# Four blocks of group 0's first layer by seven products instead of eight, in a kernel whose five queues are written out by hand, and a new order for all of it

## The chip, the cores and the metric

The kernel runs on one core of one Trainium2 chip. The metric is the time of one execution in microseconds, as the device reports it; the time before is the median of three runs. One more execution was recorded by the hardware profiler: all the single durations in this document come from it.

The core has a matrix engine (PE, with its weight loads shown apart as PEld), a vector engine (DVE), a scalar or activation engine (ACT), a general engine (POOL, which also issues some transfers) and a queue engine that only issues transfers here (SP). Each engine runs its own instructions in the order in which they are written; engines wait for each other by semaphores only.

## The reference, cut to what matters

```python
scores = scale * np.matmul(q, k.transpose(0, 1, 3, 2))      # 8 x 12 heads, 448 x 448, head width 64
attn = np.maximum(scores, 0.0) ** 2 / S                     # no softmax: relu, then square
x = attn @ v, heads joined                                  # 3584 tokens x 768
h = x @ w_in                                                # 768 x 2048
g = h * (1.0 / (1.0 + np.exp(-1.702 * h)))
out = g @ w_out                                             # 2048 x 768, float32
```

Two parts follow each other: an attention whose weights are squared relus, and two dense layers with a gate between them. All matrix products run in 16 bits.

## The kernel before

The 96 heads are cut into 24 **units** of four heads (three units make the 448 tokens of one **group**, that is, one element of the batch; there are eight groups, 0 to 7). The second layer works on **pairs** of 128-token tiles, 14 pairs in all.

The function writes helpers and then one long list of short words (lines 431 to 600). Every word issues the instructions of one helper, and since the schedule is manual, the order of the words is the order in every engine's queue. A word is a name, its arguments, after `@` the PSUM banks (P0 to P7) that it takes, and after `:` the engine (`a` ACT, `d` DVE, `p` POOL) where that is not the usual one. The words that matter:

- `Lq u`, `Lk u`: SP loads a unit's q or k in 32 bits into the only buffer of its kind; `Q u`, `K u` cast it to 16 bits (usual engine: Q on POOL, K on ACT; DVE and the others where the word says so). `jq`, `jk`, `V`, `jwa`, `jwb`, `jo` are loads issued by POOL that cast on their way (q, k of units 1 to 5, all v, the weights).
- `tq u`, `tk u`: 7 or 14 transposes on PE (lines 117, 122); `eq`, `ek` bring the result from PSUM to SBUF.
- `s u.j`: four narrow score products, 64 x 64 weights each (line 141); `r u.j.a`: relu of one 128 x 448 half (line 152 on DVE, 154 on ACT); `x u.j`: the square of both halves (line 85 on DVE, 160 on ACT); `a u`: 28 narrow products with v (line 172), which need all seven squares of the unit; `e u.s`: the result to SBUF as the token-side operand `xb` of the first layer.
- `f g.f.r`: the plain way through the first layer, used for group 0 alone. One of 16 feature blocks of 128 is 6 products of 448 columns (line 208; r = 0, 1, 2 is the unit that gives the operand). `g g.f` is the gate from PSUM (ACT), `v g.f` widens the result into `ring`, the 16-bit input of the second layer (POOL or DVE).
- `u g.i.n`: the other way, used for groups 1 to 7. Four feature blocks (i = 0 to 3) are taken together as a 2 x 2 matrix of blocks and formed by **seven products** n = 0 to 6 instead of eight (Winograd's form of Strassen's method). Each n is 6 products of 224 columns (line 188, tile `hx`). They need sums of weight blocks (`S i.n`, DVE, once for all groups) and sums of token blocks (`T g.n`, DVE, four per group, two of them in place of their operand), and between the products partial results are saved and added: `t g.i.n` copies one PSUM bank (n = 0, 2, 4; ACT or DVE) and `b g.i.n` adds a second bank to such a copy (n = 1, 3, 6; DVE). Two banks are filled in two chains: u0, t0, u2, t2, u4, t4, u5, and u1, b1, u3, b3, u6, b6. b3 needs the copy t4, b6 the copy t2. Four gates `g g.i.n` and four widenings `v g.i.n` follow.
- `A m.n`, `p m.n`, `h m.n`, `l m.n`, `o m`: the second layer of a pair, also by seven products (8 of 384 columns each, line 188, tile `ox`), with four sums on DVE, copies `h` and last steps `l` into the output tile (lines 78, 82, 357), and the store on SP. `W c.n` are its weight sums on DVE, in four parts.

So a unit's work comes in on ACT and DVE (14 relus, 7 squares), and PE mixes four kinds of work: attention of later units, first layer and second layer of earlier groups. `m1` (line 202), `unit_product` (line 246), `t_sum` (line 236) and `from_bank` (line 352, whose engine is always DVE where a half is added to the output tile) are the helpers behind the words that the prediction counts.

Of the kernel before, what the change touches and what calls it, by code (L numbers as in the profile page):

```python
# [15 lines left out]
def kernel(  # L16
# [370 lines left out]
    with tc.manual_schedule():  # L387
# [34 lines left out]
        def zeros(e, p, n):  # L422
# [8 lines left out]
            "Lq0 Lk0 z9@0 jq1 jk1 I V0 V1 z1 Q0:d z1 z1 z1 z1 z1 z1 tq0@1 K0:d eq0:a tk0@2 ek0 "  # L431
            "tq1@3 jk2 eq1 s0.1@4.5 jq2 s0.4@6.7 s0.5@0.1 r0.1.1 r0.1.0:d s0.0@2.3 jq3 r0.5.1 "
            "r0.5.0:d s0.6@5.4 r0.0.0 r0.0.1:d r0.6.0 s0.2@1.0 x0.5 r0.2.0 s0.3@2.3 tk1@5 r0.2.1 "
            "x0.1 r0.4.0 ek1 jk3 r0.3.0 x0.2 r0.6.1 s1.6@1.0 jwb0 s1.3@6.5 r0.3.1:d r1.6.0 jwa0 "
            "r1.6.1 x0.6 s1.2@2.4 s1.0@3.1 r1.3.0 x0.3 r1.2.0 s1.5@0.6 x0.0 r0.4.1 r1.5.0:d r1.2.1 "
            "s1.1@2.7 r1.0.1 r1.0.0:d tk2@0 r1.1.0 x0.4 s1.4@4.1 r1.3.1 tq2@3 ek2 r1.1.1 a0@2.5 jq4 "
            "eq2 x1.3:a x1.2 jk4 r1.5.1 r1.4.0:d tq3@0 e0.0:a V2 x1.0 s2.3@7.3 e0.1:a tk3@6 jwb2 "
            "eq3 r2.3.1 s2.2@4.2 r1.4.1 ek3 s2.1@5.0 jwa2 r2.3.0 x1.1 s3.3@3.1 r2.1.1 jwa1 s2.4@6.7 "
            "x1.6 r2.2.0 jwb1 x1.4 r3.3.1 x1.5 a1@0.4 r2.1.0 jk5 r2.4.1 r3.3.0:d r2.2.1 jq5 "
            "s2.0@1.5 r2.4.0:d s3.2@7.3 e1.1:a f0.1.0@2 V3 e1.0 r2.0.0 s2.5@6.4 r2.0.1 r3.2.1:d "  # L440
            "jwb3 s3.4@0.1 r3.2.0 f0.1.1 r2.5.1:d r2.5.0 f0.0.0@5 jwa3 x2.2 f0.0.1 r3.4.0 V4 x2.0 "
            "s2.6@3.7 r3.4.1 s3.0@4.6 r2.6.0 x2.1 tk4@0 V5 r3.0.1 f0.2.0@1 r3.0.0:d r2.6.1 jo0.0 "
# [12 lines left out]
            "x5.3 V6 f0.12.0@1 r5.6.1 K6:d f0.14.0@5 v0.4 r5.2.1 f0.12.1 r5.6.0:d Lk7 x5.0:a "
            "u1.1.0@3 x5.1 u1.0.0@2 r5.2.0 x5.6 r5.4.0 f0.13.0@0 x5.5 u1.2.0@7 e4.1:a S3.1 x5.2:a "
            "f0.12.2 x5.4 f0.14.1 g0.12 a5@4.6 S3.3 Q6:d S1.2 Lq8 tq6@1 e5.0:a v0.12:d f0.13.1 T1.1 "
            "e5.1:a f0.14.2 t1.1.0:d tk6@4 g0.14 T1.2 f0.13.2 S0.3 u1.0.1@6 g0.13 S3.2 p0.0@5 "
            "t1.0.0 v0.13 eq6:a b1.0.1 v0.14 S1.4 u1.0.2 ek6:a S3.4 u1.1.1@0 g1.0.1 T1.3 u1.3.0@1 "
            "t1.0.2 b1.1.1 v1.0.1 u1.1.2 S1.3 g1.1.1 u1.0.4 W0.1 t1.1.2 u1.0.3 W2.1 t1.0.4 u1.1.4 "  # L460
            "K7 b1.0.3 u1.1.3 W1.1 g1.0.3 Lk8 f0.9.0@4 T1.4 t1.1.4 u1.0.6 v1.0.3 Q8:a b1.1.3 f0.9.1 "
            "v1.1.1 f0.9.2 b1.0.6 Lq7 u1.1.6 W3.1 g0.9 u1.3.1@6 g1.1.3 b1.1.6 v0.9 t1.2.0 u1.1.5 "
            "v1.1.3:d t1.3.0 A0.1@0 u1.2.1@4 g1.0.6 W2.3 u1.2.2 g1.1.6 v1.0.6 b1.2.1 tk7@0 t1.2.2 "
            "u1.0.5 b1.3.1 v1.1.6 W1.3 u1.3.2 g1.3.1 W0.3 g1.2.1 u1.2.4 v1.3.1 W3.2 t1.3.2 u1.3.3 "
            "t1.2.4 u1.2.3 A0.2@1 ek7:a u1.2.5 W3.3 g1.0.5 b1.2.3 u1.3.4 K8 v1.0.5 h0.0:d tq8@0 "
            "W2.2 u1.2.6 g1.2.5 Lk9 W1.2 eq8:a p0.1@2 v1.2.5 b1.2.6 W0.2 t1.3.4 v1.2.1 W2.4 "
            "s6.0@7.0 p0.2 r6.0.0 Q7 l0.1 g1.1.5 b1.3.3 r6.0.1 V8 s6.4@4.7 Lq9 W0.4 h0.2 s6.2@3.0 "
            "p0.3 A0.3 r6.2.0 r6.4.1 W3.4 r6.2.1 W1.4 r6.4.0 s6.5@3.7 v1.1.5:d tq7@0 r6.5.0 A0.4 "
            "p0.4 r6.5.1 eq7 x6.2:a x6.5 s6.6@4.3 x6.0 h0.4 s6.3@7.0 Q9 r6.6.1 u1.3.5 r6.3.1:d "
            "r6.3.0 tk8@3 l0.3 g1.3.5 p0.5 K9:p Lq10 r6.6.0:d x6.4:a ek8 v1.3.5 Lk11 x6.3:a "  # L470
            "s7.4@0.7 l0.5 s6.1@1.4 u1.3.6 r7.4.0 r6.1.1:d o1 r7.4.1 x6.6 s7.0@3.5 s7.1@0.4 r6.1.0 "
            "p0.6 b1.3.6 r7.0.1 x6.1 r7.1.0 r7.0.0 x7.4 s7.3@7.1 r7.1.1 s7.2@6.5 l0.6 a6@0.3 r7.2.0 "
            "x7.1 o0 r7.3.0 A2.1@0 r7.2.1 s7.6@4.2 x7.0 r7.3.1 s8.4@6.7 V10 tq9@5 r7.6.0 r7.6.1:d "
            "tk9@1 Q10 e6.1:a r8.4.0:d p2.0@4 eq9:a ek9 K11:p r8.4.1:d x7.2:a s8.2@2.3 x7.6 "
            "s7.5@6.5 Lk10 p2.1@1 r7.5.1 r7.5.0:d Lq11 e6.0:a x7.3 x7.5:a r8.2.0:d s8.1@7.5 a7@6.0 "
            "r8.2.1:d r8.1.1 r8.1.0 A2.2@1 h2.0 x8.1 s8.6@2.3 s8.3@5.7 e7.0:a p2.2 r8.3.0:d e7.1:a "
            "K10:p r8.6.0 r8.6.1:d r8.3.1 l2.1 V13 s9.0@6.5 Lk12 x8.6:a s8.0@0.2 x8.3 s8.5@3.7 p2.3 "
            "r8.0.0:d r8.0.1 r9.0.1 x8.2 r8.5.1 x8.0 tk11@0 r8.5.0 u2.1.0@2 x8.4 ek11:a x8.5 a8@5.7 "
# [152 lines left out]
```

## Time and profile before

| | us |
|---|---|
| median of 3 runs | 375.39 |
| lowest, highest | 374.13, 375.76 |
| the profiled execution, its own time | 374.8 |
| its span (first to last instruction) | 373.0 |
| PE busy | 365.6 (98%) |
| DVE busy | 321.5 (86%) |
| ACT busy | 297.3 (80%) |
| POOL busy | 114.3 (31%) |
| granted PE clock | 0.998 of full speed |

The profiled execution is 0.6 us below the median of the runs and inside their spread. Its span leaves 1.8 us of its own time outside. A matmul's row is its whole passage, and the next one enters before it has left; the price of a matmul in a row of many is therefore read from start to start, not from its duration. The same holds for DVE and ACT, whose instructions overlap by about 0.1 us.

### The profile page before, as it was taken

The page shows a single profiled execution, that of the slowest core. Times are in us where ns is not written, and L with a number is a line of the kernel's source. Part 1 is how long each engine was busy: PE and PEld are TensorE (multiplying, and loading weights), DVE is VectorE, ACT ScalarE, POOL GpSimd, SP SyncE. Part 2 cuts the span into 40 slices and gives each one's busy share as a digit, 9 for nine tenths or more (in the row PEclk, how much of TensorE's full clock was granted, in tenths as well). Part 3 has the DMA queues.
Part 4 walks back from the last instruction along what each step waited for, and adds up shares of the span by engine and source line. Part 5 has one row for each costly group of instructions (what it writes and reads, how often), then busy time and mean ns, then how long its engine had stood idle before and what let it go on. Part 6 is the DMA issues. An engine that isn't in the chain of part 4 may idle for free.

```text
span 373.0 us, 9514 instructions
## 1 busy us (share of the span) xinstructions
PE 365.6 (98%) x3830; PEld 252.9 (68%) x3830; DVE 321.5 (86%) x602; ACT 297.3 (80%) x568; POOL 114.3 (31%) x164
## 2 busy tenths in 40 slices
PE   8899999999999999999999999999999999999995
PEld 4444568855589555886568965599568855788663
DVE  3999999999999998898899699978998889767762
ACT  3999989999988999789978997899994897636310
POOL 6464523452334424231341322335400410012000
PEclk9999999999999999999999999999999999999999
DMA  9999999357673437360572524620520301110344
GB/s 195 171 188 206 238 232 232 135 138 203 166 196 99 120 62 209 112 160 2 134 199 34 177 28 114 183 37 2 95 43 2 86 2 41 45 44 16 71 99 114
DMA packets 31981, 43.16 MB, mean 116 GB/s; under 512 B 2368, under 2 KB 28608, under 8 KB 31936
## 3 DMA queue, kind: packets, MB, share of 16 engines
q1 hardware_dynamic: 14928, 28.06, 25.7%
q0 software_dynamic: 16608, 14.09, 25.2%
q8 instruction: 30, 0.49, 0.5%
q10 hardware_dynamic: 400, 0.39, 0.4%
q14 instruction: 15, 0.12, 0.1%
HBM read 45.61 MB, written 11.01 MB: 152 GB/s over the span
## 4 chain that ended last, share of the span: by engine, by line
PE 95%; DVE 3%; ACT 1%; issue 0%
PE ox L188 35%; PE hx L188 30%; PE sc L141 10%; PE av L172 8%; PE ht L208 5%; PE tr L117 4%; PE zp L426 1%; DVE at L85 1%; DVE at L152 1%; PE tr L122 1%; ACT at L154 1%; DVE kT L80 0%; DVE qT L80 0%; DVE osb L357 0%; DVE wT L417 0%
## 5 line engine op out<-in xcount | busy, mean ns | idle before, releaser
L154 ACT ACTIVATE at<-sc 128x448 f16<-128x448 f32 x229 | 112.2, 567 | 10.6 <-PE sc L141 9.9
L198 POOL TENSOR_SCALAR ring<-gf 128x448 f16<-128x448 f32 x87 | 53.7, 617 | 151.0 <-ACT gf L195 144.0
L188 PE MATMUL ox<-wout,ring 128*128 128x384 f16 x448 | 80.3, 326 | 0.0
L188 PEld LDWEIGHTS <-ring 128*128 128x128 f16 x568 | 53.0, 98 | 37.5 <-issue 7.6
L152 DVE TENSOR_SCALAR at<-sc 128x448 f16<-128x448 f32 x107 | 63.9, 617 | 5.8 <-PE sc L141 5.6
L85 DVE TENSOR_TENSOR at<-at 128x896 f16<-128x896 f16 x107 | 65.5, 636 | 1.7 <-ACT at L154 1.6
L188 PEld LDWEIGHTS <-win 128*128 128x128 f16 x672 | 63.8, 98 | 4.4 <-issue 2.1
L85 DVE TENSOR_TENSOR gf<-hx,gf 128x448 f32<-128x448 f32 x84 | 50.8, 620 | 9.9 <-PE hx L188 5.2
L160 ACT ACTIVATE at<-at 128x896 f16<-128x896 f16 x61 | 57.7, 960 | 0.5
L188 PE MATMUL hx<-xb,win 128*128 128x224 f16 x504 | 57.0, 259 | 0.0
L195 ACT ACTIVATE gf<-gf 128x448 f32<-128x448 f32 x84 | 47.2, 578 | 11.5 <-DVE gf L85 11.3
L141 PE MATMUL sc<-qT,kT 64*64 64x448 f16 x672 | 50.2, 359 | 1.6 <-DVE kT L80 1.1
L188 PEld LDWEIGHTS <-winS 128*128 128x128 f16 x504 | 48.0, 98 | 3.1 <-issue 1.3
L76 ACT ACTIVATE gf<-hx 128x448 f32<-128x448 f32 x60 | 31.8, 541 | 13.4 <-PE hx L188 11.4
L188 PE MATMUL ox<-wT,asum 128*128 128x384 f16 x224 | 40.6, 327 | 0.0
L188 PE MATMUL hx<-T,winS 128*128 128x224 f16 x336 | 39.7, 259 | 0.0
L172 PE MATMUL av<-at,v 64*64 64x448 f16 x672 | 36.2, 350 | 0.1
L141 PEld LDWEIGHTS <-kT 64*64 64x64 f16 x672 | 17.1, 105 | 23.9 <-issue 17.3
L188 PEld LDWEIGHTS <-asum 128*128 128x128 f16 x224 | 20.8, 98 | 16.6 <-issue 3.4
L357 DVE SCALAR_TENSOR_TENSOR osb<-ox,osb 128x384 f32<-128x384 f32 (+1 forms) x44 | 23.8, 541 | 5.9 <-PE ox L188 5.7
L78 ACT ACTIVATE osb<-ox 128x384 f32<-128x384 f32 x26 | 13.1, 503 | 19.6 <-PE ox L188 16.8
L172 PEld LDWEIGHTS <-v 64*64 64x64 f16 x672 | 20.4, 107 | 11.6 <-issue 1.5
(61 smaller groups left out, 426.0 us busy)
## 6 DMA issues: line engine op xcount, KB each, us to landing
out_dram<-osb SPq DMA_DIRECT2D x52, 192.0 KB, 3.0
qst<-in_q_dram SPq DMA_DIRECT2D x19, 448.0 KB, 4.5
kst<-in_k_dram SPq DMA_DIRECT2D x19, 448.0 KB, 4.2
v<-in_v_dram POOLq DMA_DIRECT2D x24, 224.0 KB, 5.0
win<-in_moe_w_in_dram POOLq DMA_DIRECT2D x8, 384.0 KB, 9.7
wout<-in_moe_w_out_dram POOLq DMA_DIRECT2D x4, 768.0 KB, 20.6
q<-in_q_dram POOLq DMA_DIRECT2D x5, 224.0 KB, 5.9
k<-in_k_dram POOLq DMA_DIRECT2D x5, 224.0 KB, 5.4
```

The costliest lines, as they stand in the source:

```text
L76: nc.scalar.activation(out=o, in_=i, func=AF.Copy)
L85: eng[e].tensor_tensor(out=o, in0=x, in1=y, op=op)
L141: nc.tensor.matmul(out=sc[a][c, 0:S], lhsT=st["kT"][r, j, c], rhs=st["qT"][r, :, c], start=True, stop=True)
L152: nc.vector.tensor_scalar(out=o, in0=i, scalar1=0.0, scalar2=None, op0=ALU.max)
L154: nc.scalar.activation(out=o, in_=i, func=AF.Relu)
L160: nc.scalar.activation(out=at, in_=at, func=AF.Square)
L172: nc.tensor.matmul(out=av[s][64 * a:64 * a + 64, 0:S], lhsT=v16[r, a, 64 * j:64 * j + 64], rhs=at[r, a, :], start=(j == 0), stop=(j == J - 1))
L188: nc.tensor.matmul(out=o, lhsT=lhs(i), rhs=rhs(i), start=start and i == 0, stop=i == n - 1, skip_group_check=True)
L195: nc.scalar.activation(out=o, in_=i, func=AF.Gelu_apprx_sigmoid, scale=1.0 / SC)
L198: eng[e].tensor_scalar(out=o, in0=i, scalar1=SC, scalar2=1.0, op0=ALU.mult, op1=ALU.mult)
L208: nc.tensor.matmul(out=hp[g, f][:, 0:S], lhsT=w[:, i, fo:fo + 128], rhs=xts[g][:, i, :], start=i == 0, stop=i == NK - 1)
L357: nc.vector.scalar_tensor_tensor(out=o, in0=x, scalar=1.0 / SC, in1=o, op0=ALU.mult, op1=ALU.add)
```

## The change

Feature blocks 12 to 15 of group 0 (the fourth set of four, i = 3) are no longer formed by the plain way, but by the seven products that the other groups use. Feature blocks 0 to 11 of group 0 stay as they are. For this the list gains `u0.3.0` to `u0.3.6` with their copies, adds, gates and widenings, and the four token sums `T0.1` to `T0.4`, which group 0 did not need before. The helpers are unchanged.

All other words are the same in kind but come in a new order, with other banks, and some work has another engine: over the whole program relus go 229 to 225 on ACT and 107 to 111 on DVE, copies `t` 60 to 57 on ACT and 24 to 30 on DVE, copies `h` 26 to 29 on ACT and 17 to 14 on DVE, widenings 41 to 35 on DVE and 87 to 93 on POOL, casts of k 4 to 6 on ACT and 13 to 11 on POOL, casts of q 4 to 3 on DVE and 12 to 13 on POOL, one `eq` from ACT to DVE.

The core of the diff (the places of group 0's fourth set):

```diff
-            "S2.3 g0.7 f0.15.0@2 f0.15.1 v0.6:d r5.1.1 v0.7 S0.4 f0.15.2 r5.1.0 s5.3@0.1 g0.11 "
...
-            "x5.3 V6 f0.12.0@1 r5.6.1 K6:d f0.14.0@5 v0.4 r5.2.1 f0.12.1 r5.6.0:d Lk7 x5.0:a "
-            "u1.1.0@3 x5.1 u1.0.0@2 r5.2.0 x5.6 r5.4.0 f0.13.0@0 x5.5 u1.2.0@7 e4.1:a S3.1 x5.2:a "
-            "f0.12.2 x5.4 f0.14.1 g0.12 a5@4.6 S3.3 Q6:d S1.2 Lq8 tq6@1 e5.0:a v0.12:d f0.13.1 T1.1 "
-            "e5.1:a f0.14.2 t1.1.0:d tk6@4 g0.14 T1.2 f0.13.2 S0.3 u1.0.1@6 g0.13 S3.2 p0.0@5 "
...
+            "u0.3.0@7 r5.2.0 u1.0.0@0 S0.3 g0.5 v0.5:d r5.3.1 x5.3 x5.1 r5.2.1 x5.6 u1.1.0@1 x5.2:a "
+            "Q6:a t1.0.0:d S1.4 u1.2.0@4 T1.1 K6:p tk6@2 a5@5.3 S1.3 e4.1:a e5.0:a e5.1:a u0.3.1@6 "
+            "T1.2 tq6@5 eq6:a T1.3 u1.0.1@3 S3.1 t0.3.0:d b1.0.1 b0.3.1 t1.1.0 v0.2 u1.0.2 t1.0.2 "
+            "ek6:a p0.0@5 u1.1.2 S3.3 S3.2 h0.0 u1.1.1@2 g1.0.1 Lk7 t1.1.2 V8 v1.0.1:d S3.4 u1.0.4 "
+            "g0.3.1 v0.3.1 t1.0.4 u1.0.3 b1.1.1 g1.1.1 u1.1.4 u1.1.3 b1.0.3 t1.1.4 g1.0.3 v1.1.1 "
+            "W2.1 u1.0.6 Lq8 Q8 b1.1.3 K7 g1.1.3 b1.0.6 v1.0.3 t1.2.0 T1.4 u1.1.6 b1.1.6 W3.1 "
...
+            "u1.3.3 W0.3 Lk8 g1.2.1 t1.2.4 W3.2 u1.2.3 u1.3.2 v1.2.1 g1.3.1 T0.1 T0.2 V7 t1.3.2 "
+            "b1.2.3 W2.2 u0.3.3 T0.3 u0.3.2 v1.3.1 t0.3.2 u1.2.6 u0.3.4 K8 b1.2.6 t0.3.4 W1.2 W0.2 "
+            "tk7@0 b0.3.3 W2.3 ek7:a g0.3.3 u1.3.4 Lq7 W2.4 u0.3.6 Q7:a b0.3.6 g0.3.6 v0.3.3 tq8@0 "
+            "u1.1.5 eq8 t1.3.4 v0.3.6:d u1.2.5 g1.2.5 s6.0@6.0 r6.0.1 v1.2.5 b1.3.3 r6.0.0:d u1.3.5 "
+            "T0.4 W3.4 tq7@4 g1.1.5 v1.1.5:d W1.4 s6.2@0.6 Lq9 r6.2.1 W1.3 u0.3.5 r6.2.0 Lk9 g0.3.5 "
+            "s6.5@1.6 r6.5.1 r6.5.0 u1.3.6 s6.4@0.7 v0.3.5:d r6.4.1 p0.1@6 s6.3@1.7 g1.3.5 x6.5:a "
+            "eq7 v1.3.5 Q9 s6.6@2.4 A0.1@0 A0.2@1 p0.2 x6.2:a K9 h0.2 r6.4.0:d r6.6.1 l0.1 r6.3.0:d "
```

## The prediction

> **What bounds the kernel now.** I read the page first: its busy shares and the chain of work that ended last.
>
> ```profile
> PE 365.6 (98%) x3830; PEld 252.9 (68%) x3830; DVE 321.5 (86%) x602; ACT 297.3 (80%) x568; POOL 114.3 (31%) x164
> ...
> PE 95%; DVE 3%; ACT 1%; issue 0%
> ```
>
> The chain names PE, but rows of a matmul overlap, so 98% does not say that PE was never held up. For that I read the timeline of PE, in which runs of equal matmuls are one line (start, length, count at the end), and took every price from start to start.
>
> ```profile
> 27.36 1.49 PE L172 MATMUL av<-at,v 64*64 64x448 f16 x28
> ...
> 31.67 0.76 PE L141 MATMUL sc<-qT,kT 64*64 64x448 f16 x12
> 32.36 2.44 PE L208 MATMUL ht<-xb,win 128*128 128x448 f16 x12
> 34.74 0.76 PE L141 MATMUL sc<-qT,kT 64*64 64x448 f16 x12
> ...
> 98.26 1.55 PE L172 MATMUL av<-at,v 64*64 64x448 f16 x28
> ...
> 332.99 1.46 PE L188 MATMUL ox<-wout,ring 128*128 128x384 f16 x8
> 334.29 0.74 PE L188 MATMUL hx<-xb,win 128*128 128x224 f16 x6
> 334.87 0.74 PE L188 MATMUL hx<-T,win 128*128 128x224 f16 x6
> ...
> 366.89 1.48 PE L188 MATMUL ox<-wT,ring 128*128 128x192 f16 x16
> ```
>
> Eight second-layer products take 1.30 us (332.99 to 334.29), six first-layer products of the seven-product form 0.575. Twelve plain first-layer products take 2.38 (32.36 to 34.74) and twelve score products 0.69. Comparing runs of 4, 8 and 12, a score word of four costs 0.188 and a plain product 0.19, and each passage between narrow (64 x 64) and full matmuls adds about 0.11, so one visit to the narrow ones costs 0.22. With 28 products of an attention at 1.32, seven transposes at 0.39 (the early, narrow 14 at 0.51) and the 16 products on zeros at the start 5.3, the sum over the program is: zeros 5.3, transposes 38 x 0.39 + 10 x 0.51 = 19.9, scores 168 x 0.188 = 31.6, attention 24 x 1.316 = 31.6, plain first layer 96 x 0.19 = 18.2, seven-product first layer 196 x 0.575 = 112.7, second layer 97 x 1.30 + 2 x 0.70 = 127.5, and 66 visits x 0.22 = 14.5: 361.3 us. PE runs from 1.12 to 368.37, 367.25 us, so 5.9 us are lost. The attention of unit 2 (the line at 27.36) stands 21.3 us into that sum, but starts 26.2 us after PE did: 4.9 of the 5.9 us are lost there, and only 1.0 in the 341 us behind it. So PE is the bound without gaps from 27 us on. Who holds it in the head is DVE, and I read DVE's timeline and two stretches (columns: length, then busy us of PE, PEld, DVE, ACT, POOL, clock, DMA).
>
> ```profile
> 26.70 2.22 DVE L85 TENSOR_TENSOR at<-at 128x896 f16<-128x896 f16 x4
> 28.84 0.62 DVE L80 COPY kT<-tr 128x896 f16<-128x896 f16 x1
> ...
> 46.86 0.39 DVE L198 TENSOR_SCALAR ring<-gf 128x448 f16<-128x448 f32 x1 [0.59 <-ACT gf L195]
> ...
> 96.97 2.22 DVE L85 TENSOR_TENSOR at<-at 128x896 f16<-128x896 f16 x4
> 99.11 0.68 DVE L85 TENSOR_TENSOR ring<-ring 128x1024 f16<-128x1024 f16 x1
> ```
>
> ```profile
> 28.84:99.11 70.27, 70.26 (x767) 45.13 (x764) 67.90 (x131) 67.01 (x132) 28.25 (x37) 1.00 0.92 194
> 99.11:140.00 40.89, 40.89 (x453) 29.24 (x446) 39.17 (x74) 35.75 (x69) 16.40 (x23) 1.00 0.49 124
> ```
>
> The last square of unit 2 ends at 28.84 and that of unit 8 at 99.11. Unit 8's attention starts at 98.26 and needs its squares one by one, 0.19 us apart, so the squares come in the nick of time. In these 70.27 us DVE is idle for 2.37 us, mostly short waits for ACT as at 46.86, and ACT for 3.26. PE is the bound, with DVE 3% and ACT 5% behind it. The change lands in this stretch.
>
> **The change part by part.** *Products.* Out: 4 blocks x 6 plain products x 0.19 = 4.56 us. In: 7 x 0.575 = 4.02. PE: -0.54.
>
> *Order on PE.* Counting in the two lists of words how often a score or attention word follows a full matmul gives 66 visits before and 69 after: +3 x 0.22 = +0.66. PE's own sum ends at +0.12; 30 visits instead of 26 lie before unit 8's attention, so its place moves by 4 x 0.22 - 0.54 = +0.34, and behind it PE has 0.22 less. The Trainium skill speaks against the change here: its page "TensorEngine Tiling (Array Packing)", section Tiling Modes, says that changing the tiling mode drains the engine. It gives no price; with free passages the forecast below would be 0.7 us lower.
>
> *Work on DVE and ACT between the two attentions.* Up to unit 2's attention the counts on DVE and on ACT are equal word for word in kind, so the head is taken as unchanged; the pieces only change places, which I bound by 0.5 us either way (DVE is never idle for over 0.1 us between 7.2 and 28.8). Up to unit 8's attention, DVE gets 3 adds `b`, 3 relus and 1 copy `t` more, at 0.535 each (four squares, the same length, take 2.14 from 26.70 to 28.84): 3.75; 4 token sums `T` at 0.42 (the one at 102.40 is followed at 102.82): 1.68; it loses two casts (0.78 and 0.54) and one copy `h` (0.465): -1.79. Together +3.6. ACT gets 2 copies `t` (0.44), 3 casts (0.85), 2 copies `h` (0.41) and loses 3 relus (0.44): +2.9, which its 3.26 idle us just hold. POOL's work to there is the same.
>
> *What that does.* DVE then has 67.9 + 3.6 = 71.5 us of work for a stretch of 70.3. If it never idles, the squares of unit 8 are 1.2 us later; if its waits stay as they are, 3.6. Between these ends I take half of the idle time as gone, since a DVE that is late finds ACT and PE ready more often, yet ACT is fuller too: +2.4. PE's +0.34 is inside this, not added. Two chains belong to it as well: `u0.3.6` needs add b3, which needs copy t4 of `u0.3.4`; copy 0.54 and add 0.61 face 0.39 + 0.575 us of PE work, a shortfall of 0.2; the same chain of `u1.1.6` faces two products, 1.15, and just misses with its handovers. Queued behind a late b3 on PE are transposes and products of group 1 with their banks free, and on DVE the relus of unit 6. The first half of the pair (`p0.1`) now needs the widening of `u0.3.5`, 1.0 us of gate, widening and handovers under 1.4 us of PE work, and `p0.2` the sums `A0.1`, `A0.2` behind it, which join the same late DVE queue.
>
> *Behind unit 8.* The stretch from 99.11 to 140 leaves DVE 1.7 us idle, and up to unit 12's attention the new list puts 1.8 us more on it (0.8 + 1.0 by the same prices), while PE's part is equal. It cannot catch up at once; I add 0.5 (0 to 1.0). From unit 12 to 14 DVE has 20.7 us beside some 21 of PE, which has by then put 3 to 4 us between them; behind that DVE is below 85% by the same sums. The new list's total on DVE is +5.3, on ACT -1.0.
>
> *Widenings moved to POOL* (six, none before unit 8): 0.617 each, POOL is 31% busy, and PE reads the ring later: nothing. At 95.39 one square took 1.04 instead of 0.535 beside a cast on POOL, so six such meetings would cost DVE at most 3 us, behind unit 8, most of them where it is below 85%. The Trainium skill, "SBUF — State Buffer", section Who interferes with whom, has the same as an exclusive lock for the whole instruction; 6 x 0.617 = 3.7 by it, an estimate, with the same cover.
>
> *Transfers.* SP's loads keep their order but for neighbours that change places. In the first 80 us five of its casts stand on ACT (q6, k7, k8, q7, k9; before, three), where a late landing would hold relus and copies behind it. q6 is the tightest: its load went out at 39.55 and took 9.4 us in this trace, and the cast is due at about 49.6, 0.6 us to spare; the others have 8 us from freed buffer to cast against a median landing of 4.2 to 4.5. POOL's issues change places by one or two; the weights of the fourth set landed at 40.1 and are due at 48. Cost nothing; if a landing misses, some 1 us on ACT.
>
> *Sum.* +2.4 - 0.22 + 0.5 = +2.7. On the profiled execution (374.8) that is 377.5. It lies 0.6 under the median of the three runs, so against the median I say 375.4 + 2.7 = 378.1.
>
> **The rivals.** *It is hidden: not slower.* DVE's idle time in the 70 us is given up and unit 8 comes 1.2 us late, with nothing more behind it: 375.4 + 1.2 - 0.2 = 376.4. For it: a late engine waits less. Against: ACT has no room left, and most of DVE's waits are for ACT. It decides where DVE idles less than about 0.9 us there: then the loss stays under 0.5%, which is about what a measurement can tell from no change.
>
> *The head gets shorter: faster.* 4.9 us are lost there; an order that brings unit 2's squares 2 us earlier would give 375.4 - 2.0 + 0.1 = 373.5. Against: the same work on a DVE without gaps.
>
> *The delay piles up.* If the waits of DVE and ACT stay and the chains come on top, 3.6 + 0.5 + 1.0 - 0.2 and 1 us at ACT for a landing: 381.3. For it: ACT would be at 69.9 of 70.3.
>
> **How the numbers follow.** Forecast (loss of 1.9 to 4.5 us, 377.3 to 379.9) 0.56; hidden 0.28; head 0.07; piled up 0.09. Slower by over 0.5%: 0.56 + 0.09 = 0.65; within 0.5%: 0.28; faster: 0.07. The range goes from the floor of PE's sum with everything hidden and 0.3 for the runs, 375.4 + 0.1 - 0.3 = 375.2, to the piled-up case, 381.3; about 0.1 lies below and 0.07 above.
>
> **What would show it.** Right: unit 8's attention starts at 99.5 to 102 instead of 98.26, unit 2's stays at 27 to 28; DVE's idle share between them falls below 2%; PE shows gaps between 50 and 100 us that end at DVE (adds `gf` and squares `at`), none behind 150. Wrong: gaps on PE behind 150 us, a unit 8 at 98.6 or earlier, or a unit 2 moved by over 1 us. The forecast fails if DVE's pieces are shorter beside each other than in this trace, or if ACT, not DVE, ends the waits.

## The result and the profile after

The changed kernel takes 379.35 us, median of three runs (379.32 to 379.54), where the kernel before took 375.39 (374.13 to 375.76): the ratio is 1.0123, with a 95% interval from 1.0104 to 1.0141, so it is slower by 1.2%, 3.96 us. The profiled execution took 379.54, its span 377.8; against the profiled one before (374.8 and 373.0) that is 4.7 and 4.8 us. The difference of 0.8 between the two comparisons is the place of each profiled execution among its own runs. Two more executions of the changed kernel, taken for experiment 5, ran in a slower state, at 383.3 and 383.6 us, and are left out of every comparison.

The page of the changed kernel, its busy line and the shares of the chain that ended last:

```profile
PE 366.7 (97%) x3848; PEld 254.8 (67%) x3848; DVE 326.4 (86%) x610; ACT 296.7 (79%) x565; POOL 115.6 (31%) x169
...
PE 86%; DVE 7%; ACT 4%; issue 1%; POOL 0%; DVEq 0%
```

PE's own busy time hardly moved (365.6 before). The chain did: PE 95% became 86%, DVE 3% became 7, ACT 1% became 4. The time did not go into products but into waits. These are rows of PE's timeline, with every gap that it shows behind 22 us (start, length, tile, count; in brackets the gap and what ended it):

```profile
27.58 1.49 PE L172 MATMUL av<-at,v 64*64 64x448 f16 x28
...
39.69 0.36 PE L172 MATMUL av<-at,v 64*64 64x448 f16 x2
42.06 1.51 PE L172 MATMUL av<-at,v 64*64 64x448 f16 x26 [2.01 <-ACT gf L195]
...
63.10 0.73 PE L188 MATMUL hx<-xb,winS 128*128 128x224 f16 x6 [0.31 <-DVE gf L85]
...
70.34 1.35 PE L188 MATMUL hx<-T,winS 128*128 128x224 f16 x12 [0.20 <-DVE T L85]
...
74.48 0.73 PE L188 MATMUL hx<-xb,winS 128*128 128x224 f16 x6 [0.37 <-DVE gf L85]
...
103.50 1.52 PE L172 MATMUL av<-at,v 64*64 64x448 f16 x28
```

Unit 2's attention starts at 27.58 (27.36 before), unit 8's at 103.50 (98.26 before): 5.24 us later. The end of the span is 4.8 later, so behind unit 8 nothing more was lost, and 0.4 came back. Four gaps are seen: one of 2.01 us inside unit 3's attention that ends at a gate on ACT, and three between 60 and 75 us that end at adds (`gf`) and a token sum (`T`) on DVE.

A gap in this view is shorter than what it costs, because rows of matmuls overlap. The cost is read from start to start. Below, the time from one unit's attention to the next is set beside PE's own price for the words in between: the time that they take if nothing waits, by the prices that the prediction worked out. Unit 4's narrow transposes take 0.52 us from start to start with a score word behind them (29.00 to 29.52), no more than with a full matmul behind them in the kernel before, so no passage is counted there. The last two columns are the profiled runs of experiments 5, at 376.48 us, and 6, at 376.48 too:

| from unit to unit | price before | before | price after | after | changed kernel again | widenings on DVE |
|---|---|---|---|---|---|---|
| 2 to 3 | 11.85 | 11.75 | 12.07 | 12.11 | 12.11 | 12.11 |
| 3 to 4 | 7.44 | 7.46 | 6.93 | **9.36** | 6.97 | 6.97 |
| 4 to 5 | 5.92 | 5.91 | 4.41 | 4.41 | 4.41 | 4.41 |
| 5 to 6 | 33.21 | 33.32 | 35.35 | **37.66** | **37.77** | **37.83** |
| 6 to 8 | 12.34 | 12.46 | 12.34 | 12.38 | 12.39 | 12.39 |
| 2 to 8 | 70.76 | 70.90 | 71.10 | 75.92 | 73.65 | 73.71 |

Where nothing waits, price and trace agree within 0.12 us, passages between narrow and full matmuls included at 0.11 each. The loss of the changed kernel sits in two places: 2.4 us between units 3 and 4, and 2.3 us between units 5 and 6.

The second place is the one that the prediction spoke of. The stretches from unit 5 to unit 6 (length; then busy us of PE, PEld, DVE, ACT, POOL; clock, DMA share, GB/s), first of the kernel before:

```profile
52.48:85.80 33.32, 33.32 (x338) 24.83 (x341) 32.21 (x64) 30.36 (x59) 12.62 (x17) 1.00 0.79 189
```

and of the changed kernel:

```profile
53.46:91.12 37.66, 36.50 (x362) 27.41 (x363) 36.93 (x74) 34.28 (x65) 10.88 (x15) 1.00 0.68 158
```

DVE is idle for 0.73 of 37.66 us in the changed kernel, 1.9%.

The first place was not foreseen. The chain of waits of the changed kernel, in order of time (start, length, what):

```profile
39.54 0.37 PE sc L141 x4
40.09 0.70 POOL v L100
40.87 0.57 POOL ring L198
41.46 0.55 ACT gf L195
42.06 1.51 PE av L172 x26
```

A load of v that POOL issues (`V14`) stands at the head, then a widening on POOL, then a gate on ACT, then PE. POOL's own timeline of the changed kernel:

```profile
38.22 0.87 POOL L379 DMA_DIRECT2D wout<-in_moe_w_out_dram  x1 [0.77 <-DMA v<-in_v_dram]
40.09 0.70 POOL L100 DMA_DIRECT2D v<-in_v_dram  x1 [1.00 <-PE sc L141]
40.87 1.87 POOL L198 TENSOR_SCALAR ring<-gf 128x448 f16<-128x448 f32 x3
```

The gate's line in ACT's timeline:

```profile
41.46 0.54 ACT L195 ACTIVATE gf<-ht 128x448 f32<-128x448 f32 x1 [2.79 <-POOL ring L198]
```

The load is issued at 40.09 after a wait of 1.0 us. Three widenings (`v0.10`, `v0.3`, `v0.8`) stand behind it in POOL's queue, though their input has long been there. Until they run, the five buffers of the gate are full, so ACT's gate `g0.4` waits 2.79 us; it holds the bank that unit 3's attention takes next. The view puts the wait of the load down to PE's scores at 39.54 (`s4.4`), but that word stands behind `V14` in the list, so the load can't need it. By the waits in the program it needs the landing of the load that stands eight places before it in POOL's queue: `jwb3`, a load of weights (`win`), issued at 25.64, which landed 13.9 us later. In the profiled run of experiment 6 the view itself names a landing of `win` for the same wait. In the kernel before, the same load went out at 38.79, and of the first six widenings four stood on DVE: nothing waited.

### The profile page after: what moved, and what is told of

Its sections match the earlier page's. It is cut to its first block, busy times and chain, and to the rows that moved or that the text cites. A ratio compares the mean times of both kernels' runs of the same rounds, so it can differ in the third digit from the quotient of the medians.

```text
span 377.8 us, 9580 instructions
## 1 busy us (share of the span) xinstructions
PE 366.7 (97%) x3848; PEld 254.8 (67%) x3848; DVE 326.4 (86%) x610; ACT 296.7 (79%) x565; POOL 115.6 (31%) x169
## 4 chain that ended last, share of the span: by engine, by line
PE 86%; DVE 7%; ACT 4%; issue 1%; POOL 0%; DVEq 0%
PE ox L188 34%; PE hx L188 28%; PE sc L141 9%; PE av L172 7%; PE tr L117 4%; PE ht L208 3%; ACT at L154 3%; PE zp L426 1%; DVE at L85 1%; DVE gf L85 1%; DVE at L152 1%; DVE winS L85 1%; DVE T L85 1%; PE tr L122 1%; DVE wT L85 0%
## 5 line engine op out<-in xcount | busy, mean ns | idle before, releaser
L154 ACT ACTIVATE at<-sc 128x448 f16<-128x448 f32 x225 | 110.0, 566 | 12.7 <-PE sc L141 12.3
L198 POOL TENSOR_SCALAR ring<-gf 128x448 f16<-128x448 f32 x93 | 58.2, 626 | 151.6 <-ACT gf L195 121.9
L152 DVE TENSOR_SCALAR at<-sc 128x448 f16<-128x448 f32 x111 | 66.1, 617 | 5.7 <-PE sc L141 5.0
L188 PEld LDWEIGHTS <-win 128*128 128x128 f16 x696 | 65.7, 98 | 5.9 <-issue 3.3
L85 DVE TENSOR_TENSOR gf<-hx,gf 128x448 f32<-128x448 f32 x87 | 52.6, 619 | 11.3 <-PE hx L188 7.5
L195 ACT ACTIVATE gf<-gf 128x448 f32<-128x448 f32 x87 | 48.8, 578 | 16.8 <-DVE gf L85 16.0
L188 PE MATMUL hx<-xb,win 128*128 128x224 f16 x522 | 59.7, 259 | 0.2
L188 PEld LDWEIGHTS <-winS 128*128 128x128 f16 x522 | 49.6, 98 | 4.5 <-issue 3.0
L76 ACT ACTIVATE gf<-hx 128x448 f32<-128x448 f32 x57 | 30.5, 543 | 12.6 <-PE hx L188 10.1
L78 ACT ACTIVATE osb<-ox 128x384 f32<-128x384 f32 x29 | 14.6, 505 | 16.2 <-PE ox L188 16.2
```

Of the source, the lines that this page charges most:

```text
L76: nc.scalar.activation(out=o, in_=i, func=AF.Copy)
L85: eng[e].tensor_tensor(out=o, in0=x, in1=y, op=op)
L152: nc.vector.tensor_scalar(out=o, in0=i, scalar1=0.0, scalar2=None, op0=ALU.max)
L154: nc.scalar.activation(out=o, in_=i, func=AF.Relu)
L188: nc.tensor.matmul(out=o, lhsT=lhs(i), rhs=rhs(i), start=start and i == 0, stop=i == n - 1, skip_group_check=True)
L195: nc.scalar.activation(out=o, in_=i, func=AF.Gelu_apprx_sigmoid, scale=1.0 / SC)
```

## The experiments

Each was run beside the kernel before on the same chip, whose median there was 374.5 to 374.8.

**1. The load later in POOL's queue.**

```diff
-"... r3.5.1 g0.2 f0.1.2 x3.5 x3.3 V14 s4.3@7.6 g0.1 ..."
+"... r3.5.1 g0.2 f0.1.2 x3.5 x3.3 s4.3@7.6 g0.1 ..."
...
-"... s5.4@7.4 f0.5.1 r5.1.0:d V6 r5.5.1 ..."
+"... s5.4@7.4 f0.5.1 r5.1.0:d V14 V6 r5.5.1 ..."
```

> The changed kernel with one word moved: the load of v of unit 14 stands on POOL behind the widenings of group 0's blocks (just ahead of the load of v of unit 6) instead of ahead of them. Theory 'POOL queue': that load waits for a landing, three widenings wait behind it, ACT's gate waits for their buffer, and PE for the gate's bank; the 2.0 us gap of PE at 40 to 42 us goes and the time falls from 379.35 to 377.1 to 377.7. Rival 'DVE alone': DVE is the bound up to unit 8 anyway and the gap is only where its lateness shows; the time stays within 0.6 of 379.35. Rival 'new stop': the weights' issue right before it takes the load's place and half of the gap stays: 378.4.

Measured: 378.22 us (377.29 to 378.82), ratio 1.0093 (1.0068 to 1.0117). In the profiled run (377.29), the fastest of the four, the stop at unit 3 is gone, and unit 8's attention starts at 100.99, 2.73 later than before. What is left lies between units 5 and 6. The median is above the 377.1 to 377.7 of the theory and near the 378.4 of the rival "new stop"; whether the slower three runs had half a stop left isn't known, since none of them was profiled.

**2 and 3. The new order without the seven products.** Blocks 12 to 15 by the plain way at the places where the seven products stand, with no token sums and no adds; once as it is, once with the load moved as in 1.

```diff
-"... u0.3.0@7 ... u0.3.1@6 ... t0.3.0:d b1.0.1 b0.3.1 ..."
+"... f0.14.0@7 f0.14.1 f0.14.2 ... f0.15.0@6 f0.15.1 f0.15.2 ... g0.14 b1.0.1 g0.15 ..."
...
-"... T0.1 T0.2 V7 t1.3.2 b1.2.3 W2.2 u0.3.3 T0.3 u0.3.2 ..."
+"... V7 t1.3.2 b1.2.3 W2.2 f0.12.0@7 f0.12.1 f0.12.2 ..."
```

> The changed kernel's order, but group 0's blocks 12 to 15 by the plain way at the places of the seven products: 24 plain products instead of 42 smaller ones (PE +0.54 us), four gates and four widenings as before, and without the four token sums, three copies and three adds (DVE 3.3 to 3.8 us less, ACT 0.9 to 1.3 less). Theory 'DVE work': with the work gone, unit 8's attention starts 2 to 2.5 us earlier than in the changed kernel (at about 101.2) and the time is 377.0 to 377.8; the POOL gap stays. Rival 'order alone': the arithmetic costs nothing and the time is 379.3 to 379.9.

> Both edits of the two runs above together. If the two causes add, 375.0 to 376.0, which is the kernel before with PE's sum 0.66 us longer. If both are one and the same lateness of DVE, the time is that of the better of the two alone, 377 or more.

Measured: 380.91 us, ratio 1.0179 (1.0133 to 1.0225), and with the load moved 379.0, ratio 1.0116 (1.009 to 1.0142). With less work on DVE the new order is not faster than the changed kernel. In the second one DVE is idle for 4.6 us from unit 5 to unit 6, but PE loses as much there as in the changed kernel, part of it at waits that the plain blocks made where I put them (a widening that waits for its gate, a copy of k that comes late on ACT). So the pair is no clean test of the arithmetic. It says only that DVE's work can fall without PE's waits falling, and that the moved load was worth 1.9 us here. The stop inside unit 3's attention was 2.91 us in the first profiled run and still 1.04 in the second: there the weights' load ahead of the widenings went out only at 37.98, and the widenings started at 38.93.

**4. More DVE work in the kernel before.** Nine spare products of 128 x 672 (0.42 us each, 3.8 in all) between unit 2's and unit 8's attention.

```diff
+    spare = const("spare", [128, 672])
...
+        two["D"] = lambda e, p: tt(spare, spare, spare, ALU.mult)
...
-"... x3.1 ... x4.1 ... T1.1 ... b1.1.1 ... b1.2.1 ... b1.3.1 ... A0.2@1 ... x6.5 ... x7.1 ..."
+"... x3.1 D ... x4.1 D ... T1.1 D ... b1.1.1 D ... b1.2.1 D ... b1.3.1 D ... A0.2@1 D ... x6.5 D ... x7.1 D ..."
```

> The kernel before with nine more DVE instructions (a product of a spare tile of 128 x 672 with itself, as long as a token sum, 0.42 us each, 3.8 us in all) spread between unit 2's and unit 8's attention; nothing depends on them. Theory 'DVE work': as in the prediction, unit 8's attention comes 1.2 to 3.6 us later and the time is 376.6 to 379.0, likeliest 377.8. Rival 'hidden': DVE gives up its idle time and loses less than 1 us, 375.4 to 376.4.

Measured: 378.02 us (377.44 to 379.38), ratio 1.0095 (1.0061 to 1.0128), 3.4 us more. Unit 8's attention starts at 101.57 instead of 98.26. In the kernel before, more DVE work in this stretch costs nearly its whole length. That is the upper of the two ends that the prediction had named: DVE's idle time from unit 2 to unit 8 hardly fell (2.37 us before, 2.22 here), where the prediction took half of it as gone.

**5. The changed kernel again.** No edit.

> The changed kernel as it is, run beside the three that follow, so that they can be compared with it on one chip. It should give 1.010 to 1.014 of the kernel before again, with a stop of about 2 us of PE inside unit 3's attention (39 to 42 us), and unit 8's attention near 103.5 us. If that stop is missing in this run, it comes and goes with the landing times of the loads and can't be a fixed part of the 4 us.

Measured: 376.48, 378.73, 379.37 and 379.46 us, ratio 1.0105 (1.0075 to 1.0135). The profiled run is the 376.48, and it has no stop at unit 3. POOL's timeline in it:

```profile
36.86 0.70 POOL L100 DMA_DIRECT2D v<-in_v_dram  x1 [1.04 <-PE sc L141]
37.63 3.15 POOL L198 TENSOR_SCALAR ring<-gf 128x448 f16<-128x448 f32 x4
```

Unit 3's and unit 4's attention in PE's timeline of this run:

```profile
39.01 1.49 PE L172 MATMUL av<-at,v 64*64 64x448 f16 x28
45.98 1.49 PE L172 MATMUL av<-at,v 64*64 64x448 f16 x28
```

The same program issued the load 3.2 us earlier here, because the loads before it landed earlier; the widenings behind it ran in time, and the run took 3.06 us less than the profiled one above. So the stop is no fixed part of the change. It is a queue order that is on time with early landings and late with others.

**6. Three widenings off POOL.** The load stays where it is.

```diff
-"... g0.0 v0.10 G3 v0.3 r4.3.0:d x3.1:a ... g0.8 v0.8 x4.3 ..."
+"... g0.0 v0.10:d G3 v0.3:d r4.3.0:d x3.1:a ... g0.8 v0.8:d x4.3 ..."
```

> The changed kernel with three early widenings (v0.10, v0.3, v0.8) on DVE instead of POOL; the load V14 stays where it is in POOL's queue. Theory of POOL's queue: what holds PE inside unit 3's attention is not the load itself but the widenings behind it, whose buffers the gate on ACT waits for. Then the 2 us stop at 39 to 42 us goes, although V14 waits as long as before; DVE gets 3 x 0.39 to 0.43 = 1.2 to 1.3 us more before unit 4, of which most comes back at unit 8 if DVE has no room. So unit 3's attention runs without a stop, and the time lies 0 to 1 us below the changed kernel. Rival, that the load's data or its use of the transfer engines hold PE there: the stop stays at 1.5 us or more, and the time rises by 0.5 to 1.2.

Measured: 376.82 us (376.48 to 377.29), ratio 1.0056 (1.0041 to 1.0071), beside the changed kernel of experiment 5 on the same chip. The load went out at 38.20, between the two runs above. POOL's timeline names what it waited for, the landing of a weights' load:

```profile
38.20 0.70 POOL L100 DMA_DIRECT2D v<-in_v_dram  x1 [1.18 <-DMA win<-in_moe_w_in_dram]
```

Unit 3's attention and the ones behind it ran through in PE's timeline:

```profile
38.94 1.49 PE L172 MATMUL av<-at,v 64*64 64x448 f16 x28
45.91 1.49 PE L172 MATMUL av<-at,v 64*64 64x448 f16 x28
50.32 1.79 PE L172 MATMUL av<-at,v 64*64 64x448 f16 x28
88.15 1.49 PE L172 MATMUL av<-at,v 64*64 64x448 f16 x28
```

All four runs lie between 376.5 and 377.3, where three of four had lain at 378.7 to 379.5 with the widenings on POOL. So it is the widenings behind the load that count, not the load: the link through POOL is shown. The time fell by 2.5 us against the median of the result, more than I had put down. Between units 5 and 6 the stretch is as long as ever, 37.83.

**7. No sums and adds, load later.** The kernel leaves out the four token sums and three adds of group 0, so it doesn't compute blocks 12 to 15 as they should be. It tests whether DVE's amount of work makes the second loss.

```diff
-"... t0.3.0:d b1.0.1 b0.3.1 t1.1.0 ... g1.3.1 T0.1 T0.2 V7 ... u0.3.3 T0.3 u0.3.2 ... b0.3.3 ... b0.3.6 ... T0.4 W3.4 ..."
+"... t0.3.0:d b1.0.1 t1.1.0 ... g1.3.1 V7 ... u0.3.3 u0.3.2 ... W3.4 ..."
...
-        b = (lambda: x_block(g, 0, 0), lambda: x_block(g, 1, 0), lambda: xsum[g, 2],
+        s = (lambda n: xsum[g, n]) if g else (lambda n: x_block(g, 1, 1))
+        b = (lambda: x_block(g, 0, 0), lambda: x_block(g, 1, 0), lambda: s(2),
...
```

> The changed kernel with V14 later (as in the earlier run, 378.2) and without the DVE work that the seven products bring with them: the four token sums T0.1 to T0.4 and the three adds b0.3.1, b0.3.3, b0.3.6 are left out (the products take an unsummed block in place of a sum, the gates read the copies alone), so blocks 12 to 15 of group 0 are not what they should be. PE's and ACT's instructions and the order of all words stay. DVE has 4 x 0.42 + 3 x 0.535 = 3.3 us less between unit 2's and unit 8's attention. Theory of DVE: unit 8's attention starts 2 to 3 us earlier than with V14 later alone (100.99), at 98 to 99, and the time falls to 375.2 to 376.3. Rival, ACT (it has 2.9 us more in this stretch and keeps them here): unit 8 stays at 100.5 or later and the time within 0.7 us of 378.2. Rival, PE's own order (more changes between narrow and full matmuls): the same.

Measured: 376.4 us (376.27 to 377.35), ratio 1.0043 (1.0027 to 1.006). That is 1.8 us under experiment 1, just short of what DVE's amount asks for. But the profiled run (377.35) has unit 8's attention at 101.39, no earlier than there, and a stop of 0.54 at unit 3 although `V14` was out of the way: the weights' load ahead of the widenings went out 1.6 us later than in experiment 6. The stop follows the start of the three widenings on POOL over the profiled runs that have them there: none at 36.64 (experiment 1) and 37.63 (5), 0.54 us at 38.73 (here), 1.04 at 38.93 (3), 2.01 at 40.87 (the changed kernel). So the pair mixes both causes, and the cut is repeated in 9 on the variant in which POOL's queue holds nothing up.

**8. Four relus from DVE to ACT, load later.**

```diff
-"... r6.0.0:d ... r6.4.0:d ... r6.3.0:d ... r7.0.1:d ..."
+"... r6.0.0 ... r6.4.0 ... r6.3.0 ... r7.0.1 ..."
```

> V14 later, and four relus (r6.0.0, r6.4.0, r6.3.0, r7.0.1) moved from DVE to ACT: 4 x 0.535 = 2.1 us less on DVE and 4 x 0.44 = 1.8 more on ACT, all between unit 5's and unit 8's attention. If DVE alone is the limit there and ACT's remaining idle time (3.4 of 38.2 us in this stretch) can be used, unit 8's attention starts 1 to 2 us earlier (99 to 100) and the time falls to 376.2 to 377.2. If ACT is the limit, it gets 1 to 1.8 us slower: 379.2 to 380. If both are full and one only gives the other's load back, it stays within 0.5 us of 378.2.

Measured: 378.66 us (378.32 to 378.88), ratio 1.0104 (1.0089 to 1.0119); experiment 1 had 1.0093. No gain: from 75 us on ACT is as full as DVE, and a new gap of 0.59 us at 86 us ends at a copy (`osb`) on ACT. The waits at the adds, all ahead of 73 us, stay as they were (0.50, 0.36, 0.28 and 0.53 over the price; 0.50, 0.37, 0.29 and 0.53 in experiment 1).

**9. No sums and adds, widenings on DVE.** Words and code as in 7, on the variant of 6.

```diff
-"... t0.3.0:d b1.0.1 b0.3.1 t1.1.0 ... T0.1 T0.2 ... T0.3 ... b0.3.3 ... b0.3.6 ... T0.4 ..."
+"... t0.3.0:d b1.0.1 t1.1.0 ..."
```

> The changed kernel with the three early widenings on DVE (the earlier run of that: 376.8 with little scatter, unit 8's attention at 100.54), and again without the four token sums T0 and the three adds b0.3, so that blocks 12 to 15 of group 0 are not what they should be: 3.3 us less DVE work between unit 2's and unit 8's attention, PE, ACT and the order as they are. Cleaner than the same cut with V14 later, because there a stop from POOL's queue still stood in the profiled run. Theory of DVE's amount: PE's waits for DVE between 50 and 75 us (2.2 us over the prices) fall to under 0.5, unit 8's attention comes at 98.2 to 99.2, the time at 374.6 to 375.6. Rival, that the new order has its own chains (products n = 6 and 3 of group 1 that wait for adds and sums placed just ahead of them), which stay whatever DVE's load: 1 to 1.7 us of the 2.2 stay, unit 8 at 99.5 to 100.3, the time 375.8 to 376.6.

Measured: 376.98 us (375.98 to 380.56, ten runs), ratio 1.0062 (1.004 to 1.0084): the cut of 3.3 us DVE work gained nothing on 376.82. That is further from the theory of DVE's amount than even the rival had put it. The gaps that are left on PE:

```profile
51.59 1.33 PE L172 MATMUL av<-at,v 64*64 64x448 f16 x24 [0.70 <-DVE at L85]
60.82 0.73 PE L188 MATMUL hx<-xb,winS 128*128 128x224 f16 x6 [0.21 <-DVE gf L85]
```

Set against the price piece by piece, the four waits at adds and sums cost 1.7 us in experiment 6 (0.50, 0.37, 0.29, 0.54) and two of them remain here (0.38 and 0.29); with all the rest between unit 5's and unit 6's attention counted in, that is 0.7 us less. DVE spends the rest of the cut waiting itself, mostly for PE and ACT:

```profile
67.40 0.62 DVE L85 TENSOR_TENSOR gf<-hx,gf 128x448 f32<-128x448 f32 x1 [0.17 <-ACT gf L76]
69.63 0.62 DVE L85 TENSOR_TENSOR gf<-hx,gf 128x448 f32<-128x448 f32 x1 [1.14 <-PE hx L188]
...
73.69 0.40 DVE L198 TENSOR_SCALAR ring<-gf 128x448 f16<-128x448 f32 x1 [0.54 <-ACT gf L195]
```

In the profiled run nearly all of the 0.7 was lost again at unit 5's attention, 0.92 over the price instead of 0.30, where the kernel's words are the same as in 6. The timelines of POOL and DVE say why. POOL's in 6:

```profile
46.12 0.92 POOL L80 CAST k<-kst 128x896 f16<-128x896 f32 x1 [0.33 <-DMA kst<-in_k_dram]
```

DVE's in 6:

```profile
46.79 1.63 DVE L85 TENSOR_TENSOR at<-at 128x896 f16<-128x896 f16 x2
48.35 0.55 DVE L85 TENSOR_TENSOR winS<-winS,win 128x768 f16<-128x768 f16 x1
```

POOL's in 9:

```profile
47.19 1.19 POOL L80 CAST k<-kst 128x896 f16<-128x896 f32 x1 [1.21 <-DMA kst<-in_k_dram]
48.48 0.81 POOL L198 TENSOR_SCALAR ring<-gf 128x448 f16<-128x448 f32 x1
```

DVE's in 9:

```profile
46.97 1.89 DVE L85 TENSOR_TENSOR at<-at 128x896 f16<-128x896 f16 x2
48.78 0.91 DVE L85 TENSOR_TENSOR winS<-winS,win 128x768 f16<-128x768 f16 x1
```

The cast `K6`, which the change moved from DVE to POOL, waits for its load, and beside it and the widening behind it DVE's squares and sums take 1.89 and 0.91 us instead of 1.15 and 0.55. When k lands a microsecond later, these meet other squares, and unit 5's are later by 0.6. That is one profiled run of each kernel; whether it holds for the medians isn't shown. So the cut gained 0.7 us behind unit 5's attention, and the equal times don't prove that DVE's amount is worth nothing.

**10. Weight sums on POOL.** A way to relieve DVE that leaves nothing out; the three widenings stand on DVE as in 6.

```diff
-"... W1.2 W0.2 tk7@0 b0.3.3 W2.3 ... W2.4 u0.3.6 ... T0.4 W3.4 tq7@4 ... W1.4 ... W1.3 ..."
+"... W1.2:p W0.2:p tk7@0 b0.3.3 W2.3:p ... W2.4:p u0.3.6 ... T0.4 W3.4:p tq7@4 ... W1.4:p ... W1.3:p ..."
```

> The changed kernel with the three early widenings on DVE, and seven of the sixteen weight sums of the second layer (W1.2, W0.2, W2.3, W2.4, W3.4, W1.4, W1.3) on POOL in their places, where POOL stands idle between 68.5 and 84 us: 7 x 0.5 = 3.5 us less on DVE, nothing left out. If DVE's amount of work is what PE pays for there, and a sum on POOL takes about 1 us without holding DVE up, the waits of PE behind 68 us (0.28 + 0.54 + 0.22) go and unit 8's squares are no longer late: 0.8 to 1.2 us less, 375.6 to 376.0. Rival, that POOL's work on 16-bit tiles holds DVE (a square took 1.04 instead of 0.535 beside a cast on POOL in the profile of before): DVE gains under 1 us in sum, the second layer's first products wait for POOL, and the time is 376.8 or more.

Measured: 383.11 us (382.14 to 383.85), ratio 1.0213 (1.0192 to 1.0235): 6.3 us worse than 6. A sum took 1.65 to 1.94 us on POOL, not 1, and held DVE up. Rows of POOL's timeline in this run:

```profile
69.14 3.78 POOL L85 TENSOR_TENSOR wT<-wout,wT 128x768 f16<-128x768 f16 x2
...
78.54 3.68 POOL L85 TENSOR_TENSOR wT<-wout,wT 128x768 f16<-128x768 f16 x2
```

DVE's timeline beside it:

```profile
69.48 1.95 DVE L85 TENSOR_TENSOR xb<-xb 128x672 f16<-128x672 f16 x1
71.35 0.61 DVE L85 TENSOR_TENSOR gf<-hx,gf 128x448 f32<-128x448 f32 x1
72.91 0.62 DVE L85 TENSOR_TENSOR gf<-hx,gf 128x448 f32<-128x448 f32 x1 [0.95 <-ACT gf L76]
...
79.07 1.66 DVE L198 TENSOR_SCALAR ring<-gf 128x448 f16<-128x448 f32 x1
```

A token sum of 0.50 us took 1.95; the adds, which read one operand from PSUM, kept their 0.62. A widening, which reads a single operand from SBUF and takes 0.38 elsewhere, took 1.66. The Trainium skill, "SBUF — State Buffer", section Who interferes with whom, states that a DVE instruction with two inputs in SBUF contends with one of POOL that reads SBUF, and that one with at most one such input does not, unless it runs in one of the 2-port performance modes. The token sum and the adds agree with it; in which mode the widening ran, no view shows.

**11. Two squares of the head on POOL, in the kernel before.** For the rival of a shorter head.

```diff
-"... ek2 r1.1.1 a0@2.5 jq4 eq2 x1.3:a x1.2 jk4 ... V2 x1.0 s2.3@7.3 ..."
+"... ek2 r1.1.1 a0@2.5 x1.2:p x1.0:p jq4 eq2 x1.3:a jk4 ... V2 s2.3@7.3 ..."
```

> The kernel before with two squares of unit 1 (x1.2, x1.0) on POOL, ahead of the load jq4, where POOL stands idle (13.3 to 16.7 us): 2 x 0.535 = 1.07 us less DVE work in the head, where the prediction's rival of a shorter head lies. If DVE's amount of work sets the head, unit 2's attention starts 0.6 to 1.1 us earlier than 27.36 and the time falls by as much, to 373.6 to 374.1. If a square on POOL takes 2 us or more, or holds DVE, unit 1's attention waits for it (its first product needs x1.0): 0 to 1.5 us slower, 374.7 to 376.2.

Measured: 375.32 us (374.46 to 376.24, ten runs), ratio 1.0009 (0.9997 to 1.0022): no difference that can be measured. In its profiled run unit 2's attention starts at 27.14, 0.2 earlier. The two squares took 3.70 us on POOL, and one square of DVE beside them 1.98 instead of 0.62. POOL's timeline in this run:

```profile
14.65 3.70 POOL L85 TENSOR_TENSOR at<-at 128x896 f16<-128x896 f16 x2 [1.77 <-ACT at L154]
```

DVE's timeline beside it:

```profile
14.83 1.98 DVE L85 TENSOR_TENSOR at<-at 128x896 f16<-128x896 f16 x1
```

DVE lost 1.36 us to this one meeting, where it was to save 1.07.

**12. The same DVE work, sums behind the adds.** The widenings as in 6.

```diff
-"... u1.0.0@0 S0.3 g0.5 ... x5.6 u1.1.0@1 ... W2.1 u1.0.6 Lq8 Q8 b1.1.3 ... t1.2.4 W3.2 u1.2.3 ... b1.2.3 W2.2 ..."
+"... u1.0.0@0 g0.5 ... x5.6 S1.2 S0.3 u1.1.0@1 ... u1.0.6 Lq8 Q8 b1.1.3 W2.1 ... t1.2.4 u1.2.3 ... b1.2.3 ..."
...
-"... t0.3.4 W1.2 W0.2 tk7@0 ... Lq7 W2.4 u0.3.6 Q7:a b0.3.6 g0.3.6 ... T0.4 W3.4 ..."
+"... t0.3.4 tk7@0 ... Lq7 u0.3.6 Q7:a b0.3.6 W3.2 W2.2 g0.3.6 ... T0.4 W1.2 W0.2 W2.4 W3.4 ..."
```

> The changed kernel with the three early widenings on DVE (376.8 earlier), and eight sums that nobody waits for soon put behind the adds and squares that PE does wait for: S1.2 and S0.3 behind the last square of unit 5 (x5.6), W2.1 behind b1.1.3, W3.2 and W2.2 behind b0.3.6, W1.2, W0.2 and W2.4 behind T0.4. DVE has the same instructions, 98% busy between unit 5's and unit 6's attention as before; only their order differs, and nothing is left out. By the prices of PE that stretch is 35.35 us long; it took 37.83 with the widenings on DVE alone, 0.30 at unit 5's attention, 0.50, 0.29 and 0.54 at the products with n = 6 that wait for adds, 0.37 at a token sum. If what PE pays for is the place of the adds in DVE's queue (which the cut of 3.3 us of sums, without any gain, points to), 1.0 to 1.7 of the 2.5 us go: the stretch takes 36.1 to 36.8, unit 8's attention comes at 98.9 to 99.6, the time at 375.1 to 375.9. If it is the amount of DVE's work in this stretch, the wait comes back where the sums now stand (the first products of the second layer, the scores and squares of unit 6): the stretch stays above 37.4 and the time within 0.5 us of 376.8.

Measured: 380.42 us (380.19 to 381.5), ratio 1.0157 (1.0138 to 1.0175), 3.6 us worse than 6, and neither theory had put it there. The waits at the adds did not go (0.36 twice in the gaps), and new ones came where the sums now stand. One of them, read backwards from PE through ACT to DVE. PE's timeline of this run:

```profile
81.88 0.38 PE L141 MATMUL sc<-qT,kT 64*64 64x448 f16 x3 [0.78 <-ACT gf L195]
```

ACT's:

```profile
81.29 0.54 ACT L195 ACTIVATE gf<-hx 128x448 f32<-128x448 f32 x1 [1.18 <-DVE ring L198]
```

DVE's:

```profile
78.94 1.95 DVE L85 TENSOR_TENSOR wT<-wout,wT 128x768 f16<-128x768 f16 x4
80.81 0.38 DVE L198 TENSOR_SCALAR ring<-gf 128x448 f16<-128x448 f32 x1
```

Four sums stand ahead of a widening, the gate behind the widening has no buffer, and the scores of unit 6 have no bank. The same amount of work on a queue that was 98% full cost 3.6 us more in another order, because a piece that is put back stands ahead of something that another engine waits for; the one case is shown here, the others were not followed.

No variant of the changed kernel beats the kernel before; the best that computes everything is the sixth, 376.82.

## Why the prediction was right, and where it was not

- **Direction and size.** Slower by 2.7 was said, and 3.96 came. The sum was short by one term that it did not have. That the time still lies inside the forecast's 377.3 to 379.9 is in part luck: in its one profiled run without the stop the changed kernel took 376.48, below that span, and in the other runs compared here 378.73 to 379.54. The part that the prediction did price measures 2.1 us in experiment 6 (376.82 beside 374.72).
- **Products and passages.** Right. The price from unit 2 to unit 8 is 71.10 after and 70.76 before, 0.34 more (the prediction had +0.34 up to unit 8), and wherever nothing waits the trace agrees with it within 0.12 us. With free passages these sums would not close, and 0.11 us for each is what this kernel pays. The Trainium skill, "TensorEngine Tiling (Array Packing)", section Tiling Modes, says that a change of mode drains the engine; the sums agree with it. The prediction's remark that free passages would make its forecast 0.7 us lower doesn't follow from its own sum: the +0.34 was inside the +2.4, so only the -0.22 behind unit 8 would have changed.
- **The head.** Right: unit 2's attention moved by 0.22 us, inside the 0.5 that was allowed (and by 0.46 the other way in experiment 5). Experiment 11 found no shorter head either.
- **DVE ends PE's waits between 50 and 100 us.** Right in place and engine: three gaps at `gf`, `T` and `gf`, none behind 150. Right in size too, but only without the stop at unit 3: then unit 8's attention starts at 100.54 to 100.99 (experiments 1, 5 and 6), 2.3 to 2.7 later, where +2.4 was taken. In the profiled run it started at 103.50, outside the 99.5 to 102 that was to show the forecast right. The other sign, a DVE idle for under 2% from unit 2 to unit 8, was missed as well. It held from unit 5 to unit 6 alone (1.9%); over the whole stretch DVE was idle for 4.01 us (5.3%) in the profiled run and 1.87 (2.5%) in that of experiment 5, beside 2.37 (3.3%) before. The two stretches, the changed kernel and experiment 5 (columns as above):

```profile
27.58:103.50 75.92, 72.74 (x793) 47.04 (x785) 71.91 (x139) 69.27 (x134) 27.66 (x38) 1.00 0.90 178
```

```profile
26.90:100.55 73.65, 72.55 (x794) 46.87 (x787) 71.78 (x139) 69.34 (x134) 28.43 (x37) 1.00 0.87 180
```

- **Its working failed in part.** The step *What that does* priced the loss as DVE's added work less half of its idle time. Experiment 4 gives its upper end, nearly the whole of the added work; experiments 9 and 12 don't fit. With 3.3 us of that work gone the time stayed, and with the same amount in another order it rose by 3.6. What is seen (in experiment 6) is 1.7 us at four adds and sums that PE needs within one or two products, 0.3 at unit 5's squares and 0.2 at scores. The step had two of the four as an afterthought, at 0.2 and "just misses"; they cost 0.54 (`u0.3.6`) and 0.50 (`u1.1.6`). How much of the loss the amount alone makes stays open, between nothing (6 against 9) and 1.8 us (1 against 7, which ran on two chips and beside stops of different length); no order that frees these adds was found.
- **ACT "just holds" its extra work.** Right for the change: ACT was not what ended the waits at 60 to 75 us. Its busy time between the two attentions rose by 1.7 us (67.64 to 69.34 in experiment 5) and not by the 2.9 of the sum, with 4.3 us left idle there. Behind 75 us there was nothing to spare: four more relus (experiment 8) made a new wait.
- **"POOL's work to there is the same" and *Transfers*: "Cost nothing".** This step failed. The count of widenings per engine is equal up to unit 8, but which of them stand on POOL is not. Three that a gate waits for had come to stand behind a load whose own wait depends on other landings. That cost 2.4 us in the profiled run, none in the 376.48 run. The prediction had looked at POOL's issues as transfers that might come late, not as waits that hold POOL's arithmetic, and it had allowed 1 us for a missed landing, on ACT.
- **+0.5 behind unit 8.** Not found; 0.4 came back.
- **Casts.** `K6` on POOL was counted as 0.78 us less on DVE. The squares beside it take part of that back, 0.5 to 1.1 us, more when k lands late. The prediction had this meeting only for widenings behind unit 8. No run puts `K6` back on DVE by itself, so what the move costs in time isn't shown.

## What to carry to other kernels

When work changes queues, count per engine is not enough: list what stands behind each instruction that waits for a transfer, and who waits for that. On an engine that is full to a few per cent, price the waits of the bound engine one by one, by the distance between a product and the add that it needs; the sum of the work only says that there is no room to repair them. If one program's runs differ by 3 us, look at the landing times of its loads before explaining a difference.

## What the runs showed of the hardware

- A load that POOL issues can wait, in this program, for the landing of an earlier, unrelated load, and POOL's arithmetic behind it waits with it: issue at 40.09 or 36.86 us in two runs of one program, 379.54 or 376.48 us.
- Arithmetic on POOL is no spare room beside a DVE that works on two 16-bit operands in SBUF: 0.62 became 1.98 us, 0.50 became 1.95, while adds with one operand in PSUM kept 0.62. A widening with its one operand in SBUF was held too, 1.66 instead of 0.38 beside sums on POOL. A sum of 128 x 768 takes 1.65 to 1.94 us on POOL and 0.55 on DVE.
